# Attention with sinks and routed experts on one core: transpositions of P on half of the array, the sinks' exponentials apart from P, x stored in whole rows

## The chip, the cores and the metric

One of the eight cores of a Trainium2 chip runs the kernel. A core has TensorE (matmuls and weight loads, results in PSUM), VectorE, ScalarE, GpSimd and SyncE, which here issues transfers; in the profile they are PE and PEld, DVE, ACT, POOL and SP. The metric is the device time of one execution in microseconds.

## The reference

Causal attention in a window of 128 positions, to which the first four positions (the sinks) are always added, and behind it a layer of eight experts. An expert takes 384 of the 3072 tokens, in the order of the routing logits.

```python
batch, n_heads, seq, head_dim = (4, 8, 768, 64); n_sink, window = (4, 128)
scores = scale * np.matmul(q, k.transpose(0, 1, 3, 2))
keep = is_sink | in_window
scores = np.where(keep, scores, -1000000000.0)
a = np.exp(scores - np.max(scores, axis=-1, keepdims=True))
a = a / (np.sum(a, axis=-1, keepdims=True) + 1e-09)
x = np.matmul(a, v)                    # (B, H, S, D), then (B*S, H*D)
logits = x @ w_gate                    # N=3072, D=512, E=8
# each token goes to its best expert that still has room (cap = N // E)
h = np.maximum(x[mask] @ w1[e], 0.0)   # F=1024
out[mask] = h @ w2[e]
```

All data are float32.

## The kernel before

Attention comes first, then routing and experts (class `Moe`); x goes between them through DRAM (`x_dram`), the logits through the SBUF tensor `L`.

Attention works in 24 chunks of 128 queries, six for each of four batches. A chunk `c` passes these steps; `g` is one of two halves of the heads, so most of them come twice a chunk.

- `ldq`, `ldk`, `lv`: SyncE loads q, k and v, four chunks ahead. In `kk` a block of 128 keys has the four sinks' keys in front of it, `W=132` columns.
- `qs` (GpSimd, L74): q times 0.125.
- `QK` (TensorE, L83): the scores into a PSUM tile `pp`, as 64x64 matmuls on the four quarters of the array. Because one query half of 64 sees the keys from its own diagonal back, a row has 64 columns of an older block, 64, the 4 sinks, and 64.
- `cp` (VectorE, L89 to L93): triangles of the two diagonal blocks are merged into 64 columns by a predicated copy; `mx` (L94) takes the maximum.
- `e` (ScalarE, L99): the exponentials of 132 columns of a head into `P`, with their sum into `sm`.
- `T` (TensorE, L107): the 64x64 blocks of P are transposed by matmuls with an identity; `pe` (ScalarE, L108) copies them into `PT`.
- `A`, `B` (GpSimd, L110, L111): the merged diagonal block is split into its two triangles, `E` and what stays in `PT`.
- `ss` (ScalarE, L114): two copies, one for each half of the queries, take the sinks' columns of P into `ss`, a tile that holds zeros for the other batches. `Ts` (TensorE, L118) transposes them, `pS` (ScalarE, L119) copies them.
- `AV` (TensorE, L129): PT and E times v. `ae` (VectorE, L132) copies it.
- `X` (TensorE, L136, L138): the sinks' part of the result, and the product with `iw`, which is an identity beside the gate's weights, so that 64 columns of x and 8 of logits come out for a head.
- `ra`, `r` (VectorE): 1 / (sum + 1e-9); `xe` (L140) multiplies by it and writes `xt`; `lm` (L142) adds the logits over the heads; `xo` (SyncE, L143) stores x.

Each step is a function `op_...`. Their order on each engine is not that of a loop: `schedule()` simulates all steps with costs in ns (`table`), the latencies `LAT`, rings of buffers (`buffers`: how many slots a tensor has, and which step frees one) and an offset for each step (`OFF`), and `plan_of` sorts the steps by the start so found. `attention` then issues them in that sequence. All PSUM tiles of attention are four slots `pp` of two banks, one step to a slot.

An f32 matmul of the program is issued as two passes, each of them a weight load and a matmul.

## Time and profile before

| | |
|---|---|
| three runs | 545.25 us median, 541.69 to 548.64 |
| the profiled execution | 545.01 us |
| its span, first to last instruction | 543.3 us |
| instructions in it | 16,624, of them 6873 matmuls and 6873 weight loads |
| TensorE's mean granted clock | 0.96 of 2.4 GHz |
| busy of the span: PE, PEld, DVE, ACT, POOL | 86%, 74%, 65%, 44%, 32% |

A time is that of one execution on the device; the span is what the trace covers of it. The shares are means over attention, routing and experts, which differ; each has to be read on its own. Matmuls overlap, so that a busy PE is not one at its peak. A wait is put down to what came last before the waiting instruction; "issue" is idle time for which the trace shows no releaser.

### The profile page before, as it was taken

The page shows a single profiled execution, that of the slowest core. Times are in us where ns is not written, and L with a number is a line of the kernel's source. Part 1 is how long each engine was busy: PE and PEld are TensorE (multiplying, and loading weights), DVE is VectorE, ACT ScalarE, POOL GpSimd, SP SyncE. Part 2 cuts the span into 40 slices and gives each one's busy share as a digit, 9 for nine tenths or more (in the row PEclk, how much of TensorE's full clock was granted, in tenths as well). Part 3 has the DMA queues.
Part 4 walks back from the last instruction along what each step waited for, and adds up shares of the span by engine and source line. Part 5 has one row for each costly group of instructions (what it writes and reads, how often), then busy time and mean ns, then how long its engine had stood idle before and what let it go on. Part 6 is the DMA issues. An engine that isn't in the chain of part 4 may idle for free.

```text
span 543.3 us, 16624 instructions
## 1 busy us (share of the span) xinstructions
PE 468.9 (86%) x6873; PEld 400.3 (74%) x6873; DVE 352.7 (65%) x1040; ACT 237.2 (44%) x690; POOL 174.0 (32%) x231
## 2 busy tenths in 40 slices
PE   7777776877777478898999998999999989999995
...
GB/s 237 201 171 167 167 140 159 160 160 167 83 74 51 32 117 246 8 187 220 21 303 85 61 326 40 74 276 79 79 329 21 180 373 184 58 21 54 25 6 53
DMA packets 75085, 73.23 MB, mean 135 GB/s; under 512 B 28033, under 2 KB 57601, under 8 KB 75009
## 3 DMA queue, kind: packets, MB, share of 16 engines
...
q8 instruction: 54, 0.88, 0.7%
q14 instruction: 23, 0.18, 0.1%
HBM read 59.57 MB, written 12.58 MB: 133 GB/s over the span
## 4 chain that ended last, share of the span: by engine, by line
PE 57%; DMA 15%; DVE 12%; issue 10%; ACT 2%; POOL 2%; SPq 1%; POOLq 0%; ACTq 0%; DVEq 0%
PE ph L680 16%; PE py L692 15%; DMA raw<-w 12%; PE pp L129 6%; PE pp L83 5%; PE pp L107 5%; PE pp L138 2%; PE pp L136 2%; PE pr L543 2%; DVE wl L654 2%; DVE cmp L473 2%; PE pt L667 1%; DMA xg<-x_dram,idx 1%; DVE hl L684 1%; DMA us<-ud 1%
## 5 line engine op out<-in xcount | busy, mean ns | idle before, releaser
L652 ACT ACTIVATE wh<-raw 128x1024 fp32r<-128x1024 f32 x64 | 67.8, 1060 | 76.9 <-DMA raw<-w 38.9
L680 PE MATMUL ph<-xh,wh 128*128 128x384 f32 x256 | 92.3, 360 | 4.0 <-DVE hl L684 4.0
L654 DVE TENSOR_TENSOR wl<-raw,wh 128x1024 fp32r<-128x1024 f32 x64 | 77.7, 1220 | 23.2 <-ACT wh L652 22.9
L680 PE MATMUL ph<-xl,wh 128*128 128x384 f32 x256 | 88.1, 344 | 0.0
L680 PE MATMUL ph<-xh,wl 128*128 128x384 f32 x256 | 88.0, 344 | 0.0
L692 PE MATMUL py<-wh,hh 128*128 128x512 f32 x192 | 79.9, 416 | 2.2 <-ACT yo L695 2.2
L697 POOL DMA_INDIRECT out<-yo,idx x24 | 26.7, 1114 | 166.9 <-ACT yo L695 113.4
L659 POOL DMA_INDIRECT xg<-x_dram,idx x24 | 33.3, 1389 | 139.5 <-issue 49.5
L692 PE MATMUL py<-wh,hl 128*128 128x512 f32 x192 | 75.9, 395 | 0.0
L692 PE MATMUL py<-wl,hh 128*128 128x512 f32 x192 | 75.8, 395 | 0.0
L99 ACT ACTIVATE P<-pp,nmx 128x132 f32<-128x132 f32 x192 | 69.0, 372 | 7.9 <-DVE nmx L94 6.6
L683 ACT ACTIVATE hh<-ph 128x384 fp32r<-128x384 f32 x64 | 31.2, 488 | 82.3 <-PE ph L680 61.7
L684 DVE SCALAR_TENSOR_TENSOR hl<-ph,hh 128x384 fp32r<-128x384 f32 x64 | 35.3, 553 | 39.7 <-ACT hh L683 39.1
L107 PE MATMUL pp<-idt,P 64*64 64x64 f32 x1536 | 39.6, 226 | 23.5 <-issue 23.5
L680 PEld LDWEIGHTS ph<-xh,wh 128*128 128x128 f32 x256 | 50.2, 196 | 7.1 <-DVE hl L684 5.1
L107 PEld LDWEIGHTS pp<-idt,P 64*64 64x64 f32 x1536 | 35.0, 140 | 24.0 <-issue 23.5
L110 POOL TENSOR_TENSOR E<-PT,me 128x256 f32<-128x256 f32 x48 | 35.7, 744 | 49.2 <-ACT PT L108 48.6
L680 PEld LDWEIGHTS ph<-xl,wh 128*128 128x128 f32 x256 | 49.6, 194 | 2.0
L680 PEld LDWEIGHTS ph<-xh,wl 128*128 128x128 f32 x256 | 49.6, 194 | 0.0
L83 PE MATMUL pp<-kk,q 64*64 64x196 f32 (+2 forms) x768 | 44.5, 327 | 4.8 <-issue 3.5
L108 ACT ACTIVATE PT<-pp 128x512 f32<-128x512 f32 x48 | 28.6, 597 | 33.1 <-PE pp L107 32.9
L692 PEld LDWEIGHTS py<-wh,hh 128*128 128x128 f32 x192 | 36.9, 192 | 7.6 <-ACT yo L695 2.6
...
## 6 DMA issues: line engine op xcount, KB each, us to landing
...
v<-vd SPq DMA_DIRECT2D x24, 256.0 KB, 3.8
x_dram<-xt SPq DMA_DIRECT2D x24, 256.0 KB, 3.1
...
q<-qd SPq DMA_DIRECT2D x23, 256.0 KB, 4.9
xg<-x_dram,idx POOLq DMA_INDIRECT x24, 5.8
out<-yo,idx POOLq DMA_INDIRECT x24, 2.8
...
```

Source lines behind the costliest of these rows:

```text
L83: PE.matmul(sp[o,s,196*u+a:196*u+196],q[p,g+2*u,o],kk[p,g+2*u,k0+64*f+a:k0+64*f+196],start=True,stop=True)
L99: A.activation(T('P',c)[:,h,:],sp[:,s,u,64:196],AF.Exp,bias=T('nmx',c)[:,b:b+1],scale=1.0,accum_out=T('sm',c)[:,h:h+1])
L107: for u in range(2): PE.matmul(t[half(u),s,128*x+64*l:128*x+64*l+64],T('P',c)[half(s),2*(g+2*u)+x,a:a+64],idn[half(s),half(s)],start=True, ...
L110: def op_A(c,g): G.tensor_tensor(T('E',c)[:,2*g:2*g+2],diag(c,g),me[:,None].to_broadcast([128,2,2,64]),OP.mult)
L129: PE.matmul(av[half(s),u,a:a+64*n],T('v',c-w)[half(u),256*l+64*x:256*l+64*x+64],m.rearrange("p a n->p (a n)"),start=g==0 and n==2 and w==0 ...
L652: g.add('A',947,lambda wh=wh,raw=raw: nc.scalar.activation(wh,raw,AF.Copy),[f'raw{q}'],[f'wh{s}'],f'H{k}.{j}',f'W{k}')
L654: g.add(e,{'V':1135,'P':2303}[e],lambda wh=wh,wl=wl,raw=raw,e=e: (nc.vector if e=='V' else nc.gpsimd).tensor_tensor(wl,raw,wh.bitcast(F32) ...
L659: g.add('P',1038,lambda t=t: nc.gpsimd.indirect_dma_start(out=self.xg[t],out_offset=None,in_=self.x_dram,in_offset=bass.IndirectOffsetOnAx ...
L680: nc.tensor.matmul(p[:,0:CAP],x[:,c,:],y[:,c,:],start=c==0 and i==0,stop=c==3 and i==2)
L683: g.add('A',371,lambda f=f,p=p: nc.scalar.activation(self.hh[:,f,:],p[:,0:CAP],AF.Relu),ps,[f'hh{f}'],f'hh{k}.{f}',f'H{k}')
L684: g.add('V',469,lambda f=f,p=p: nc.vector.scalar_tensor_tensor(self.hl[:,f,:],p[:,0:CAP],0.0,self.hh[:,f,:].bitcast(F32),op0=OP.max,op1=OP ...
L692: nc.tensor.matmul(p,x[:,f,ts],w,start=f==0 and i==0,stop=f==7 and i==2)
```

## The change

Three things are done, and the plan is computed anew for them.

First, `T`. P is laid out so that two heads' blocks of 64 columns lie side by side, and one transposition takes both: 64 rows and 128 columns of the array, written to all 128 partitions, instead of two f32 matmuls with the identity. `Ts` does the same.

Second, the sinks. They are no longer part of P. The keys lie as 4 sinks, 64 keys, 4 sinks, 64 keys (`W=136`), so that every query half finds the sinks between its two blocks of scores. A new step `sd` on VectorE subtracts the maximum from the four columns, `ss` is one exponential on ScalarE from there, with no copy from P; a new step `rs` on VectorE sums the sinks' exponentials, and `ra` adds that to the sum of the rest.

Third, `xt` holds 512 columns of x and behind them 64 of logits. `xe` writes them with two instructions, and `xo` stores rows of 2 KB where it stored pieces of 256 bytes.

`schedule()` gets new costs, a cost for changes of the array's shape (`SWITCH`), and for each 256 instructions of TensorE a least distance (`INS`, `FETCH`); `OFF` is a new table, of which the diff shows one line.

```diff
-W=132
+W=136
...
-    for n,sh,dt in (('v',[128,512],F32),('P',[128,H,W],F32),('nmx',[128,H],F32),('sm',[128,H],F32),('PT',[128,4,4,64],F32),('E',[128,4,2,64],F32),
-                    ('pS',[128,128],F32),('r',[128,H],F32),('at',[128,HP,128],F32),('xt',[128,H,72],F32)):
+    for n,sh,dt in (('v',[128,512],F32),('P',[128,4,2,2,64],F32),('sd',[128,2,HP,4],F32),('nmx',[128,H],F32),('sm',[128,H],F32),('PT',[128,4,4,64],F32),('E',[128,4,2,64],F32),
+                    ('pS',[128,128],F32),('r',[128,H],F32),('at',[128,HP,128],F32),('xt',[128,576],F32)):
...
-                    p,o=half(s),half(f); a=0 if i else 64 if f else 128
-                    PE.matmul(sp[o,s,196*u+a:196*u+196],q[p,g+2*u,o],kk[p,g+2*u,k0+64*f+a:k0+64*f+196],start=True,stop=True)
+                    p,o=half(s),half(f); a=0 if i else 68 if f else 132; k0=(i-1)*W+4+68*f
+                    PE.matmul(sp[o,s,200*u+a:200*u+200],q[p,g+2*u,o],kk[p,g+2*u,k0+a:k0+200],start=True,stop=True)
...
+    def op_sd(c,g):
+
+        V.tensor_tensor(T('sd',c)[:,:,g::2,:],scores(c,g)[:,:,:,132:136],nmx(c,g)[:,:,:,None].to_broadcast([128,2,2,4]),OP.add)
     def op_e(c,x):
         g,u=x//2,x%2; sp=scores(c,g)
         for s in range(2):
             h=2*(g+2*u)+s; b=4*g+2*s+u
-            A.activation(T('P',c)[:,h,:],sp[:,s,u,64:196],AF.Exp,bias=T('nmx',c)[:,b:b+1],scale=1.0,accum_out=T('sm',c)[:,h:h+1])
+            A.activation(T('P',c)[:,2*g+s,:,u,:],sp[:,s,u,64:200].rearrange("p (a n)->p a n",a=2)[:,:,4:68],AF.Exp,bias=T('nmx',c)[:,b:b+1],scale=1.0,accum_out=T('sm',c)[:,h:h+1])
     def op_T(c,g):
 
         t=T('p',c,f'T{g}')
         for x in range(2):
             for l in range(2):
                 for s in range(2):
-                    a=((68,0),(4,68))[s][l]
-                    for u in range(2): PE.matmul(t[half(u),s,128*x+64*l:128*x+64*l+64],T('P',c)[half(s),2*(g+2*u)+x,a:a+64],idn[half(s),half(s)],start=True,stop=True)
+                    PE.transpose(t[:,s,128*x+64*l:128*x+64*l+64],T('P',c)[half(s),2*g+x,1-(l^s)].rearrange("p u n->p (u n)"),idn[half(s),half(s)])
...
-    def op_ss(c):
-        for f,a in ((0,64),(1,0)): A.activation(ss(c)[half(f),:,c//NB],T('P',c)[half(f),:,a:a+4].rearrange("p (h s) k->p s h k",s=2),AF.Copy)
+    def op_ss(c): A.activation(ss(c)[:,:,c//NB],T('sd',c),AF.Exp)
     def op_Ts(c):
         t=T('p',c,'Ts'); x=ss(c).rearrange("p s b h k->p (s b h k)")
         for s in range(2):
-            for r in range(2): PE.matmul(t[half(r),s,0:64],x[half(s),half(r)],idn[half(s),half(s)],start=True,stop=True)
+            PE.transpose(t[:,s,0:64],x[half(s)],idn[half(s),half(s)])
...
-    def op_ra(c): V.tensor_scalar(T('r',c),T('sm',c),1e-9,None,op0=OP.add)
+    def op_rs(c): V.tensor_reduce(T('r',c).rearrange("p (j s)->p s j",s=2),ss(c)[:,:,c//NB],AX.X,OP.add)
+    def op_ra(c): V.scalar_tensor_tensor(T('r',c),T('r',c),1e-9,T('sm',c),op0=OP.add,op1=OP.add)
...
-        V.tensor_tensor(T('xt',c).rearrange("p (j s) n->p s j n",s=2),T('p',c,'X')[:,:,0:288].rearrange("p s (j n)->p s j n",j=4),
-            T('r',c).rearrange("p (j s)->p s j",s=2)[:,:,:,None].to_broadcast([128,2,4,72]),OP.mult)
...
+        for a,b,n in ((0,64,0),(64,72,512)):
+            V.tensor_tensor(T('xt',c)[:,n:n+8*(b-a)].rearrange("p (j s n)->p s j n",s=2,j=4),x[:,:,:,a:b],r.to_broadcast([128,2,4,b-a]),OP.mult)
...
+    def op_xo(c): nc.sync.dma_start(x_dram[c*128:(c+1)*128,:],T('xt',c)[:,0:512])
...
-    add('ss','A',260,ae+[('~zs',1-NB)])
-    add('ra','V',75,ae)
+    add('ss','A',140,[('sd0',0),('sd1',0)]+[('~zs',1-NB)])
+    add('rs','V',100,[('ss',0)])
+    add('ra','V',75,ae+[('rs',0)])
...
+                if ins[0]>=256:
+                    w=max(0,ins[1]+FETCH-(t1-cost*(ins[0]-256)/INS[k])); t1+=w; ins[1]=t1-cost*(ins[0]-256)/INS[k]; ins[0]-=256
...
-SWITCH=dict(nr=90,rn=200)
+SWITCH=dict(nr=90,rn=200,nt=90,tn=200,rt=100,tr=200)
+INS=dict(QK0=32,QK1=32,T0=16,T1=16,Ts=4,AV0=64,AV1=64,X=80,U=16); FETCH=4300
...
-OFF={'A0': 18335, 'A1': 52415, 'AV0': 14908, 'AV1': 84106, 'B0': 47216, 'B1': 7783, 'QK0': 2872, 'QK1': 4297, 'T0': 8328, 'T1': -8153, 'Ts': 15650, 'U': -22652, 'Uc': -13081, 'cp0': -10470, 'cp1': 78107, 'e0': 58010, 'e1': 95573, 'e2': 687, 'e3': 927, 'fi': 95598, 'lm': -9483, 'mx0': 14597, 'mx1': -49747, 'pS': 60593, 'pe0': 61206, 'pe1': -9424, 'pr0': 95367, 'pr1': -19606, 'pr10': -47988, 'pr11': 79834, 'pr12': 60010, 'pr13': -8724, 'pr14': 3651, 'pr15': 2764, 'pr2': 75294, 'pr3': -25455, 'pr4': 59901, 'pr5': -70, 'pr6': 12471, 'pr7': 98043, 'pr8': -8311, 'pr9': 6044, 'qs': 50785, 'r': 61220, 'ra': -6513, 'ss': 79894, 'um': 11705, 'xe': -10955, 'xo': -20341, 'zs': -5463, 'pr16': -102190, 'ae': -9891, 'X': -32988}
```

TensorE in the midst of attention, before (a row is a matmul of the program, `x16` sixteen alike; `pp_...` is a PSUM slot; `kk,q` is QK, `idt,P` T, `vx,pS` and `iw,at` X, `PT,v` and `E,v` AV, `idt,ss` Ts):

```order
L83 MATMUL pp_214<-kk,q_166 64x196 x8
L107 MATMUL pp_216<-idt,P_245 64x64 x16
L136 MATMUL pp_215<-vx,pS_263 64x288 x4
L138 MATMUL pp_215<-iw,at_270 64x72 x16
L107 MATMUL pp_213<-idt,P_245 64x64 x16
L83 MATMUL pp_216<-kk,q_166 64x196 x8
L129 MATMUL pp_215<-PT_256,v_241 64x128 x4
L129 MATMUL pp_215<-PT_256,v_239 64x128 x4
L129 MATMUL pp_215<-E_259,v_239 64x64 x4
L129 MATMUL pp_215<-E_259,v_241 64x64 x4
L118 MATMUL pp_213<-idt,ss_2_232 64x64 x4
```

The same place after:

```order
L130 MATMUL pp_213<-PT_259,v_240 64x128 x4
L130 MATMUL pp_213<-PT_259,v_241 64x128 x4
L130 MATMUL pp_213<-E_263,v_241 64x64 x4
L130 MATMUL pp_213<-E_263,v_240 64x64 x4
L138 MATMUL pp_216<-vx,pS_266 64x288 x4
L140 MATMUL pp_216<-iw,at_272 64x72 x16
L109 MATMUL pp_214<-idt,P_245 128x64 x8
L82 MATMUL pp_213<-kk,q_162 64x200 x8
L109 MATMUL pp_214<-idt,P_245 128x64 x8
L119 MATMUL pp_216<-idt,ss_2_229 128x64 x2
L82 MATMUL pp_215<-kk,q_162 64x200 x8
```

X has left its place between the two T; the second T has Ts right behind it, and the two AV stand together, so that the array's shape changes four times a chunk: before and behind the first T, and around the second with Ts.

VectorE, before, from one `xe` to the next:

```order
L140 TENSOR_TENSOR xt_272<-pp_215,r_267 128x2x4x72
L142 TENSOR_REDUCE L<-xt_272 128x8
L89 COPY_PREDICATED pp_213<-mprev,pp_213 128x2x2x64
L94 TENSOR_REDUCE nmx_250<-pp_213 128x4
L132 COPY at_270<-pp_215 128x512
L89 COPY_PREDICATED pp_214<-mprev,pp_214 128x2x2x64
L94 TENSOR_REDUCE nmx_249<-pp_214 128x4
L130 TENSOR_SCALAR r_267<-sm_254 128x8
L131 RECIPROCAL r_267<-r_267 128x8
```

The same place after, as far as the next `xe`:

```order
L144 TENSOR_TENSOR xt_276<-pp_215,r_267 128x2x4x64
L144 TENSOR_TENSOR xt_276<-pp_215,r_267 128x2x4x8
L131 TENSOR_REDUCE r_268<-ss_1_231 128x2x4
L145 TENSOR_REDUCE L<-xt_276 128x8
L88 COPY_PREDICATED pp_213<-mprev,pp_213 128x2x2x64
L94 TENSOR_REDUCE nmx_253<-pp_213 128x4
L88 COPY_PREDICATED pp_215<-mprev,pp_215 128x2x2x64
L97 TENSOR_TENSOR sd_248<-pp_213,nmx_253 128x4x4
L94 TENSOR_REDUCE nmx_253<-pp_215 128x4
```

The step `sd` (L97) stands behind the copy of the next scores, not right behind its own maximum; `rs` (L131) has come in, and `xe` is two rows.

## Rows read from the trace of the kernel before

**Rows 1.** Busy times of two stretches, from the first restart of TensorE after a gap to the routing, and from there to the end. Columns: the stretch, its length, then for each engine the busy time and (x) its instructions, the granted clock of TensorE as a share of 2.4 GHz, the share of the DMA engines, GB/s.

```profile
18.64:176.08 157.44, 117.34 (x4670) 106.94 (x4670) 102.86 (x233) 105.64 (x468) 101.63 (x128) 0.99 0.49 135
176.08:543.30 367.22, 337.30 (x1985) 284.49 (x1984) 241.41 (x787) 122.50 (x184) 60.06 (x48) 0.95 0.37 128
```

**Rows 2.** What TensorE's matmul row waited for in attention: engine, tile and line, the releaser, us in total, times, longest.

```profile
PE pp L107 <- issue: 23.5, 17, 2.2
PE pp L138 <- issue: 5.4, 4, 1.9
PE pp L129 <- issue: 4.8, 9, 1.2
PE pp L83 <- issue: 3.5, 3, 2.3
PE pp L129 <- POOL PT L111: 1.0, 1, 1.0
```

**Rows 3.** Busy times of stretches, each from one restart of TensorE after a gap of issue to a later one; columns as in rows 1. First single ones, then longer ones (of 8, 10, 11 and 5 such steps), and the whole.

```profile
83.46:88.56 5.10, 2.83 (x129) 2.62 (x129) 2.77 (x8) 3.71 (x17) 4.06 (x5) 1.00 0.71 202
...
102.44:106.68 4.24, 3.42 (x127) 3.09 (x127) 2.78 (x6) 2.99 (x14) 3.17 (x7) 1.00 0.76 195
...
140.16:144.05 3.89, 3.04 (x128) 2.72 (x127) 2.11 (x5) 2.95 (x12) 2.44 (x3) 1.00 0.09 21
...
18.64:53.15 34.51, 25.00 (x1018) 22.59 (x1018) 22.06 (x49) 24.89 (x112) 26.49 (x32) 1.00 0.55 158
58.25:102.44 44.19, 32.73 (x1274) 29.94 (x1274) 27.30 (x60) 30.19 (x133) 29.98 (x41) 0.96 0.53 148
102.44:148.15 45.71, 35.32 (x1401) 32.01 (x1401) 31.39 (x67) 32.61 (x145) 31.51 (x39) 1.00 0.53 143
148.15:168.83 20.68, 15.55 (x637) 14.32 (x637) 13.83 (x38) 13.80 (x61) 8.91 (x13) 1.00 0.27 67
...
18.64:168.83 150.19, 111.98 (x4457) 102.08 (x4457) 98.04 (x222) 104.59 (x465) 99.83 (x126) 0.99 0.51 140
```

**Rows 4.** The page's part on DMA queues: queue and kind, packets, MB, share of 16 engines; the row of TensorE's instruction blocks.

```profile
q8 instruction: 54, 0.88, 0.7%
```

**Rows 5.** Groups of instructions by line up to 220 us, shapes kept apart: T (L107) and Ts (L118), matmuls (PE; weight loads have rows of their own, PEld, with the same counts). Columns: line, engine, operation, out<-in, rows*columns of the array, moving or loaded operand, xcount | busy us, mean ns of one | idle before.

```profile
L107 PE MATMUL pp<-idt,P 64*64 64x64 f32 x1536 | 39.6, 226 | 23.5 <-issue 23.5
...
L118 PE MATMUL pp<-idt,ss 64*64 64x64 f32 x192 | 9.1, 222 | 1.5 <-ACT P L99 0.9 <-issue 0.7
```

**Rows 6.** Timeline of TensorE's matmuls in a stretch with no gap, nearly a chunk: start us, us from the first start to the last end, line, tiles, shape, count.

```profile
97.45 0.61 PE L129 MATMUL pp<-PT,v 64*64 64x128 f32 x16
...
98.11 0.29 PE L118 MATMUL pp<-idt,ss 64*64 64x64 f32 x8
98.23 0.61 PE L129 MATMUL pp<-PT,v 64*64 64x128 f32 x16
...
98.90 0.84 PE L83 MATMUL pp<-kk,q 64*64 64x196 f32 x16
99.57 0.64 PE L107 MATMUL pp<-idt,P 64*64 64x64 f32 x32
100.03 0.66 PE L136 MATMUL pp<-vx,pS 64*64 64x288 f32 x8
...
101.02 0.28 PE L107 MATMUL pp<-idt,P 64*64 64x64 f32 x6
```

**Rows 7.** Transpositions of f32 in the expert stage (L667): the weight loads of those that write to pt, 90 of 96 (ns, min/median/max), and six of them in the timeline.

```profile
L667 PEld LDWEIGHTS pt<-idt,xg x90: 138/140/229, 204.2 to 464.4; 128*128 128x128 f32 x90
...
409.17 0.85 PE L667 MATMUL pt<-idt,xg 128*128 128x128 f32 x6
```

**Rows 8.** Timeline of TensorE's weight loads at two changes between 64x64 and the full array, and the group of L69's loads.

```profile
6.78 0.33 PEld L149 LDWEIGHTS <-const-float32-0.0 128*128 128x128 bf16 x3 [0.18 <-issue]
...
11.11 0.42 PEld L69 LDWEIGHTS pp<-us 128*128 128x128 f32 x3
11.55 0.21 PEld L83 LDWEIGHTS pp<-kk,q 64*64 64x64 f32 x8
...
L69 PEld LDWEIGHTS pp<-us 128*128 128x128 f32 x8 | 1.0, 191 | 2.1 <-DMA us<-ud 2.1
```

**Rows 9.** Groups of the other engines in attention (columns as in rows 5): GpSimd, ScalarE's sink copy, VectorE's nearest small ones.

```profile
L110 POOL TENSOR_TENSOR E<-PT,me 128x256 f32<-128x256 f32 x48 | 35.7, 744 | 49.2 <-ACT PT L108 48.6
...
L74 POOL TENSOR_SCALAR q<-q 128x512 f32<-128x512 f32 x23 | 34.5, 1501 | 4.1 <-DMA q<-qd 4.1
...
L114 ACT ACTIVATE ss<-P 64x32 f32<-64x32 f32 x48 | 10.7, 222 | 0.3
...
L142 DVE TENSOR_REDUCE L<-xt 128x8 f32<-128x64 f32 x24 | 6.5, 269 | 0.6
...
L90 DVE COPY_PREDICATED pp<-m,big 128x16 f32<-128x16 int32 x8 | 1.7, 214 | 0.3
```

**Rows 10.** DMA issues of the page: what, KB each, us to landing.

```profile
x_dram<-xt SPq DMA_DIRECT2D x24, 256.0 KB, 3.1
```

**Rows 11.** The clock: busy times of two stretches (columns as in rows 1), and the start of T in the second in the timeline; X runs from 93.64 us to there.

```profile
86.29:93.64 7.35, 3.03 (x129) 2.90 (x127) 4.34 (x11) 3.46 (x18) 4.08 (x5) 1.00 0.53 148
93.64:97.08 3.44, 3.44 (x82) 2.86 (x85) 1.06 (x3) 2.06 (x8) 1.45 (x2) 0.51 0.02 5
...
95.57 1.09 PE L107 MATMUL pp<-idt,P 64*64 64x64 f32 x32
```

More of the change, by code (lines that the diff above doesn't have):

```diff
@@ L77, in op_QK @@
         i=c%NB; q=qs[c%NQ]; sp=T('p',c,f'QK{g}')
-        k0=(i-1)*W+4 if i else -128
         for u in range(2):
@@ L159, in layouts @@
     sk=np.broadcast_to(kT[:,:,:,None,:4],(B,H,64,NB,4))
-    kd=pairs(np.concatenate([sk,kT.reshape(B,H,64,NB,128)],-1))
+    kb=kT.reshape(B,H,64,NB,2,64)
+    kd=pairs(np.concatenate([sk,kb[:,:,:,:,0],sk,kb[:,:,:,:,1]],-1))
     vd=v.reshape(B,2,4,NB,2,64,64).transpose(1,5,0,3,4,2,6).reshape(128,B,NB,512)
@@ L186, in table @@
     for h in range(2):
-        add(f'QK{h}','E',lambda c: 660 if c%NB else 445,[('ldk',0),('ldk',-1),('qs',0)]+[(f'{n}{x}',0) for x in ((0,1),(2,))[h] for n in ('qs.','ldk')])
+        add(f'QK{h}','E',lambda c: 675 if c%NB else 445,[('ldk',0),('ldk',-1),('qs',0)]+[(f'{n}{x}',0) for x in ((0,1),(2,))[h] for n in ('qs.','ldk')])
         add(f'cp{h}','V',lambda c: 335 if c%NB>1 else 490 if c%NB else 670,[(f'QK{h}',0)])
         add(f'mx{h}','V',615,[(f'cp{h}',0)])
-        for u in range(2): add(f'e{2*h+u}','A',697,[(f'mx{h}',0)])
+        add(f'sd{h}','V',95,[(f'mx{h}',0)])
+        for u in range(2): add(f'e{2*h+u}','A',690,[(f'mx{h}',0)])
     ae=[(f'e{h}',0) for h in range(4)]
     for g in range(2):
-        add(f'T{g}','E',490,[(f'e{2*g}',0),(f'e{2*g+1}',0),('ldn',0)])
+        add(f'T{g}','E',250,[(f'e{2*g}',0),(f'e{2*g+1}',0),('ldn',0)])
         add(f'pe{g}','A',479,[(f'T{g}',0)])
@@ L197, in table @@
     add('zs','P',lambda c: 480 if c%NB==1 and c//NB<B-1 else None,[('B1',0)])
-    add('ss','A',260,ae+[('~zs',1-NB)])
-    add('ra','V',75,ae)
+    add('ss','A',140,[('sd0',0),('sd1',0)]+[('~zs',1-NB)])
+    add('rs','V',100,[('ss',0)])
+    add('ra','V',75,ae+[('rs',0)])
     add('r','V',120,[('ra',0)])
-    add('Ts','E',130,[('ss',0),('ldn',0)])
+    add('Ts','E',65,[('ss',0),('ldn',0)])
     add('pS','A',230,[('Ts',0)])
@@ L210, in table @@
     add('X','E',980,[('ae',0),('pS',0),('um',0),('ldi',0)])
-    add('xe','V',680,[('X',0),('r',0)])
+    add('xe','V',740,[('X',0),('r',0)])
     add('lm','V',135,[('xe',0)])
@@ L267, in schedule @@
                 for x in rs: readers[x,c].append((t,k,c))
-    et=collections.defaultdict(float); et['E']=3700.0; mode=['n']; out=[]; ld=[]; fills=[]; dq=[0.0]
+    et=collections.defaultdict(float); et['E']=3700.0; mode=['n']; ins=[100,0.0]; out=[]; ld=[]; fills=[]; dq=[0.0]
     def dma(t,dur):
@@ L321, in schedule @@
             if e=='E':
-                md='n' if k=='U' else 'r'
-                t1+=SWITCH.get(mode[0]+md,0); mode[0]=md
+                md='n' if k=='U' else 't' if k[0]=='T' else 'r'
+                t1+=SWITCH.get(mode[0]+md,0); mode[0]=md; ins[0]+=INS[k]//(2 if k[:2]=='AV' and c%NB==0 else 1)
+                if ins[0]>=256:
+                    w=max(0,ins[1]+FETCH-(t1-cost*(ins[0]-256)/INS[k])); t1+=w; ins[1]=t1-cost*(ins[0]-256)/INS[k]; ins[0]-=256
             if e=='E' and s<60000 and s-et[e]>400:
@@ L764, in attention_general @@
                     sp=ps.tile([128,384],F32,name="sp",bufs=2)
-                    nc.tensor.matmul(sp,q[hs,h//2,:],kT[hs,h//2,3*g:3*g+3,4:W],start=True,stop=True)
+                    nc.tensor.matmul(sp,q[hs,h//2,:],kT[hs,h//2,3*g:3*g+3].rearrange("p b (l w)->p b l w",l=2)[:,:,:,4:68],start=True,stop=True)
                     nc.scalar.activation(sc[:,384*g:384*g+384],sp,AF.Copy,scale=0.125)
```

30 lines of the change are left out of this document (16 added, 14 removed).

## The prediction

> **What bounds the kernel now.** The change touches only the attention stage, so I read its length first. By the busy times of two stretches [rows 1] it ends near 176 us, where the routing begins; the 367.22 us behind that are expert work, whose code is the same. In attention the matmul row of TensorE is busy 117.34 of 157.44 us and no other engine more, so none is full. The next view is what TensorE waited for [rows 2]: hardly any of it is another engine (GpSimd has most, 1.0 us). Nearly all is "issue", idle time with no releaser: 23.5 + 5.4 + 4.8 + 3.5 us and some smaller, about 38 us.
>
> What "issue" is shows when stretches are cut from one restart of TensorE after such a gap to the next [rows 3]. Whatever lies in them, matmuls and weight loads together come to 254 to 258, and each stretch takes 3.89 to 5.10 us though the matmuls are busy in only 2.83 to 3.42 us of it. A gap every 256 instructions is no dependency of the program. The table of DMA queues has the partner [rows 4]: 54 instruction packets of 0.88 MB together, 16 KB each, and 13,746 matmuls and weight loads are 54 times 256. So TensorE runs through a block of 256 instructions and then stands until the next has been fetched. The last row of [rows 3] holds 35 blocks: 150.19 us / 35 = **4.29 us a block**, which is what sets the pace of attention. Its 8914 counted instructions are 255 a block; the rest are semaphore instructions, which that view leaves out.
>
> **The change, part by part.** *Transposes.* Before, T costs 1536 matmuls and as many loads in 24 chunks, 64 + 64 a chunk, Ts 8 + 8 [rows 5]: an f32 matmul is issued as two passes of a load and a matmul. A transposition of the array is one load and one matmul: L667 makes 12 for each of 8 experts, 90 of the 96 into pt, and these have 90 loads [rows 7]. The new T makes 8 of them for each half of a chunk, Ts 2: 32 + 4 instructions instead of 128 + 16. That is 108 fewer a chunk; a full chunk of 416 comes to 308 by my count (the title says 304, which I don't find).
>
> *Blocks.* The chunk that lies before 18.64 us is left out. 23 chunks x 108 / 255 = 9.7 blocks fewer, x 4.29 us = **41.8 us less**, if each block still takes 4.29 us. About 27 blocks are left to attention. The four stretches at the foot of [rows 3] hold 8, 10, 11 and 5 blocks: 4.31, 4.42, 4.16 and 4.14 us a block. With 4.14 for all the time falls by 4 us more, with 4.42 by 3.5 us less; I take the mean.
>
> *What is late next.* A full chunk of 308 instructions is 1.21 blocks, 5.18 us by the fetch. On the array a chunk now takes 4.70 us where nothing stops it [rows 6]: two AVs and Ts 1.45 us (97.45 to 98.90), one QK 0.67, one T 0.46, X 0.99 (100.03 to 101.02), and QK and T once more. Without T and Ts (0.92 + 0.12) that is 3.66 us. The new T isn't in the trace. Nearest is L667, six f32 transpositions in 0.85 us of which the last lasts 0.27 [rows 7]: 0.116 us each, on the full array with 128 columns. Eight one behind the other would be 0.93 us; but the new ones take turns between the two halves of the array's rows, as the old four-way ones overlap in quarters, and at two at a time they take 0.46 us, the old figure. At the old pace per instruction (0.46 us for 32 pairs) they would be 0.12 us. I take 0.46 us; two and a Ts are 1.04 us. New, too, is the change of shape, 64x64 to 64x128 and back, four a chunk by the order above. The nearest rows change between the full array and 64x64 [rows 8]. Into the full array the loads stand still for 0.18 us ahead of 6.78 us. Out of it, three loads fill 11.11 to 11.53 us, each 0.19 us long, so they start 0.115 us apart and the last at 11.34; the next starts at 11.55 us, 0.21 us later, so 0.10 us are lost. Four cost 0.40 to 0.72 us; nothing of the trace excludes 0. I take 0.5 us. Then the array needs 3.66 + 1.04 + 0.5 = 5.2 us a chunk, as much as the fetch. Of a fetch of 4.29 us TensorE idles 1.4 us now, which swallows every late input; that cover is gone afterwards.
>
> *The other engines* [rows 9]. GpSimd keeps its work: 1.50 + 4 x 0.74 = 4.46 us a chunk (L111 is as long as L110). ScalarE loses one of two sink copies (0.22 us), and its exponentials are 128 columns wide, not 132. VectorE gets two sd, one rs and a second piece of xe; the nearest rows are 0.22 us (L90, 16 columns in PSUM) to 0.27 us (L142), so about 0.9 us more on the 102.86 us / 23 chunks = 4.5 us that it is busy now [rows 1]. Those 5.4 us overlap in part (a next instruction starts before the recorded end of the last), but on ss, rs, ra and r now hangs xe, which frees the PSUM tile of X, and sd is one reader more that has to leave the tile of QK. All three engines would be 75 to 95% busy in a chunk of 5.5 us.
>
> Two demands of 5.2 us a chunk that vary (blocks from 3.89 to 5.10 us), with three engines close behind, don't give 5.2 us together. My estimate is 0.25 us a block over the fetch, 4.54 us, that is 5.5 us a full chunk: 27 x 0.25 = **6.8 us given back**. Its ends are 0 and the array's upper bound, which is a rival.
>
> *The x store.* 24 transfers in pieces of 256 bytes land in 3.1 us [rows 10]; now 2 KB each. The store lies on no wait of [rows 2]; that the last rows arrive sooner ends beside the routing, and the gathers that read them start at 199 us. Fewer packets may shorten the fetch, which shares the DMA engines: at most the 4 us above. The keys grow from 528 to 544 bytes a piece, 3%. I take 0 for both.
>
> **Sum.** The profiled execution took 545.01 us, span 543.3 us; the median of the three runs is 545.25, so the two need no correction. 545.0 - 41.8 + 6.8 = **510.0 us**. The bounds of the terms: 545.0 - 41.8 = 503 without anything given back, 499 with blocks of 4.14 us.
>
> **Rivals.** *The array becomes the bound.* Transpositions that don't overlap (2 x 0.93 + 0.23 us) and changes of shape at 0.18 us each make 3.66 + 2.09 + 0.72 = 6.47 us a full chunk. From 18.64 us on there are 23 chunks; the four of 24 that open a batch have half the AV, 64 instructions fewer, so a mean chunk is 297.3 / 308 = 0.965 of a full one. 23 x 0.965 x 6.47 = 143.6 us, 13.8 us less than the 157.44 us of now: 531 us. For it: the two rows of another shape are all there is. Against: the 32 pairs of the old T, on four quarters of the array, take 0.46 us together [rows 6], so pieces of the array do overlap. Chance 0.17.
>
> *Another engine or a chain sets the pace.* GpSimd at 4.46 us plus its waits for ScalarE, or VectorE with its additions, at 6.0 us a full chunk: 23 x 0.965 x 6.0 = 133.2 us, 521 us. Against: before the change they deliver whenever a block comes early, after 3.89 us. Chance 0.08.
>
> *The clock falls; slower.* The row of the clock is 1.00 through nearly all of attention; it was 0.51 (1.2 GHz instead of 2.4) from 93.64 to 97.08 us, after a stretch with TensorE busy 3.03 of 7.35 us [rows 11]. At that clock X takes 1.93 us (93.64 to 95.57) for 0.99: 1.9 times as long. If the new mix ran at 1.2 GHz throughout, a chunk would be 1.9 x 5.2 = 9.9 us, 23 x 0.965 x 9.9 = 220 us, the end at 607 us; it costs more than the fetch gives back from about a third of the time at that clock on. Against it: the matmuls that stay, 3.66 us, come in a shorter chunk than now, so they stand closer. Chance 0.04. The Trainium skill speaks for this rival ("TensorE: Matmul & The Clock Gate", Part 4: PE-mode transpose): it says that the full clock isn't engaged by transpositions. No run here shows a long row of them.
>
> *The gaps are no fetch; slower.* If their cause lay elsewhere and 38 us of gaps stayed, fewer instructions would save nothing, and the array's 5.2 instead of 4.70 us a chunk would add 23 x 0.5 = 11.5 us: 556 us. Against it stands the count of 256. Chance 0.03. The Trainium skill has it so ("Runtime: NRT & Kernel Launch", Instruction fetch mechanics): it holds that TensorE's instructions are read in 16 KB blocks and that this is hidden, since instructions are issued more slowly than blocks arrive. The size agrees with [rows 4], the hiding does not: 4.29 us a block against 2.9 us of work (256/416 of 4.70). By that sentence the time would be 545 us or above.
>
> **How the numbers follow.** The forecast, 499 to 518 us, has 0.65; the array 0.17, another engine 0.08, the clock 0.04, no fetch 0.03, and 0.03 is for what I don't see. The range is 499 to 524 us: it holds the forecast, the engine case and the lower part of the array case. Two per cent, about what a measurement of this kernel tells from no change, is 534 us. Faster by that has 0.65 + 0.08 and most of the array case, 0.89 in all; within 2% the rest of it, 0.05; slower 0.06.
>
> **What the profile after would show.** Instruction packets fall from 54 to about 44. The routing begins near 141 us, not 176. "Issue" on TensorE falls to less than half of 38 us, and between restarts there are still 256 instructions, at 4.1 to 4.6 us a block. T with its eight matmuls takes 0.4 to 0.5 us with its gaps at the changes of shape beside it; GpSimd is the fullest of the others. If T stands at 0.9 us and the gaps at its edges at 0.2 us, the array case holds; if the clock's digits in attention fall, that one; if the gaps no longer come at every 256th instruction but the time is the same, my reading of them is wrong.

## The result and the profile after

The changed kernel takes **518.34 us** (median of 4 runs, 517.38 to 518.71) where the kernel before took 546.19 us in runs on the same chip (median of 4): a ratio of 0.950, with a 95% interval from 0.943 to 0.956. It is faster by 5%, inside the range of the forecast (499 to 524 us), 8.3 us above the forecast of 510.0 us and 0.3 us above the 499 to 518 us that had most of the chance. The profiled execution took 518.64 us, its span is 516.9 us.

The two stretches of [rows 1], cut again at the routing, show where the time went. Columns: stretch, length, then busy time and (x) instructions of TensorE's matmuls, its weight loads, VectorE, ScalarE and GpSimd, the granted clock, DMA share, GB/s.

```profile
18.64:152.36 133.72, 114.91 (x3445) 92.47 (x3435) 112.85 (x325) 98.98 (x447) 99.53 (x128) 1.00 0.52 160
152.36:516.90 364.54, 335.77 (x1985) 283.55 (x1985) 241.18 (x787) 122.39 (x184) 62.90 (x48) 0.96 0.37 129
```

Attention ends 23.7 us earlier (152.36 us, not 176.08). The rest is 2.7 us shorter, though its code is the same; with that code it took between 364.4 and 371.9 us in the profiled executions below, so this difference is no effect of the change. TensorE's matmuls are now busy for 86% of attention (75% before), VectorE for 84% (65%). The clock stayed at 1.00, that is 2.4 GHz.

The row of instruction packets [rows 4]:

```profile
q8 instruction: 44, 0.72, 0.6%
```

The stops of the kernel before follow these packets. Between 18.64 and 176.08 us its trace puts 30 idle times of TensorE's matmuls of 0.3 us or more down to "issue", and each of them ends 1.2 to 1.6 us after an instruction packet has arrived. In the changed kernel four are left, 1.4 to 1.5 us after a packet.

And what TensorE's matmuls waited for in attention, the view of [rows 2] (releaser: us in total, times, longest):

```profile
PE pp L109 <- ACT P L102: 10.1, 13, 1.5
PE pp L119 <- DVE at L134: 1.9, 1, 1.9
PE pp L109 <- DVE xt L144: 1.4, 3, 0.5
PE pp L82 <- issue: 1.3, 4, 0.5
PE pp L140 <- issue: 0.7, 1, 0.7
PE pp L130 <- issue: 0.7, 1, 0.7
```

"Issue" was 38 us and is now under 3. In its place stands a wait that was not there: T (L109) waits 10.1 us for ScalarE's exponentials (P, L102).

T itself, in the timeline of TensorE (start us, us from first start to last end, line, shape, count; before: [rows 6]):

```profile
85.48 0.46 PE L109 MATMUL pp<-idt,P 64*128 64x64 f32 x8
85.78 0.23 PE L119 MATMUL pp<-idt,ss 64*128 64x64 f32 x2
85.93 0.91 PE L82 MATMUL pp<-kk,q 64*64 64x200 f32 x16
...
88.64 0.46 PE L109 MATMUL pp<-idt,P 64*128 64x64 f32 x8
89.03 0.89 PE L82 MATMUL pp<-kk,q 64*64 64x200 f32 x13
```

Eight transpositions, then Ts 0.30 us later (so, or a little sooner, in 9 of the 14 cases up to 142 us; 0.40 to 0.75 us in the others), and the next 64x64 work 0.16 to 0.21 us after Ts. Where 64x64 work follows T itself, it starts 0.39 to 0.40 us behind T's start in 9 of 18 cases, later in the others.

### The profile page after: what moved, and what is told of

The parts are those of the page before. It is cut to its first block, busy times and chain, and to the rows that moved or that the text cites. A ratio compares the mean times of both kernels' runs of the same rounds, so it can differ in the third digit from the quotient of the medians.

```text
span 516.9 us, 14206 instructions
## 1 busy us (share of the span) xinstructions
PE 465.7 (90%) x5577; PEld 383.8 (74%) x5577; DVE 362.9 (70%) x1136; ACT 229.8 (44%) x666; POOL 175.7 (34%) x231
## 4 chain that ended last, share of the span: by engine, by line
PE 46%; DVE 16%; DMA 15%; ACT 5%; issue 3%; POOL 1%; SPq 0%; POOLq 0%; ACTq 0%; DVEq 0%
PE ph L689 17%; PE py L701 16%; DMA raw<-w 12%; ACT P L102 3%; PE pp L82 3%; DMA xg<-x_dram,idx 3%; PE pr L552 2%; PE pp L130 2%; PE pt L676 2%; DVE cmp L482 2%; PE pp L109 1%; DVE wl L663 1%; DVE nmx L94 1%; DVE hl L693 1%; ACT wh L661 1%
## 5 line engine op out<-in xcount | busy, mean ns | idle before, releaser
L706 POOL DMA_INDIRECT out<-yo,idx x24 | 28.0, 1167 | 163.9 <-ACT yo L704 115.1
L668 POOL DMA_INDIRECT xg<-x_dram,idx x24 | 34.9, 1453 | 139.0 <-issue 48.3
L102 ACT ACTIVATE P<-pp,nmx 128x128 f32<-128x128 f32 x192 | 68.4, 369 | 20.1 <-DVE sd L97 10.7
L82 PE MATMUL pp<-kk,q 64*64 64x200 f32 (+2 forms) x768 | 44.8, 333 | 2.9 <-issue 1.3
L112 POOL TENSOR_TENSOR E<-PT,me 128x256 f32<-128x256 f32 x48 | 35.4, 744 | 26.3 <-ACT PT L110 25.4
L701 PEld LDWEIGHTS py<-wh,hl 128*128 128x128 f32 x192 | 36.0, 188 | 8.1
L704 ACT ACTIVATE yo<-py 128x512 f32<-128x512 f32 x24 | 14.3, 597 | 57.4 <-PE py L701 42.4
L102 ACT ACTIVATION_READ_ACCUMULATOR P<-pp,nmx 128x1 f32 x192 | 39.4, 205 | 0.0
```

The lines of the kernel that those rows point to most:

```text
L82: PE.matmul(sp[o,s,200*u+a:200*u+200],q[p,g+2*u,o],kk[p,g+2*u,k0+a:k0+200],start=True,stop=True)
L102: A.activation(T('P',c)[:,2*g+s,:,u,:],sp[:,s,u,64:200].rearrange("p (a n)->p a n",a=2)[:,:,4:68],AF.Exp,bias=T('nmx',c)[:,b:b+1],scale=1. ...
L112: def op_A(c,g): G.tensor_tensor(T('E',c)[:,2*g:2*g+2],diag(c,g),me[:,None].to_broadcast([128,2,2,64]),OP.mult)
L668: g.add('P',1038,lambda t=t: nc.gpsimd.indirect_dma_start(out=self.xg[t],out_offset=None,in_=self.x_dram,in_offset=bass.IndirectOffsetOnAx ...
L701: nc.tensor.matmul(p,x[:,f,ts],w,start=f==0 and i==0,stop=f==7 and i==2)
L704: g.add('A',478,lambda p=p,y=y: nc.scalar.activation(y,p,AF.Copy),ps,[f'yo{n%3}'],f'y{k}.{t}',f'Y{k}')
```

## The cost of sd, in the rows of after

ScalarE's waits for VectorE in attention, and VectorE's wait the other way (releaser: us in total, times, longest):

```profile
ACT P L102 <- DVE sd L97: 10.3, 25, 0.9
ACT P L102 <- DVE nmx L94: 8.4, 12, 1.2
...
DVE sd L97 <- ACT P L102: 6.5, 15, 0.7
```

The exponentials wait for sd, and sd waits for exponentials, though neither reads what the other writes. What they share is what they read: the maximum, and the PSUM tile of the scores. By these waits whichever engine comes second in the written order waits until the other has read. That it is the PSUM tile and not the maximum, the runs below show. One such place in the timeline (start us, duration, engine, line, [idle before <- releaser]):

```profile
74.06 0.71 DVE L94 TENSOR_REDUCE nmx<-pp 128x4 f32<-128x528 f32 x1
...
74.68 0.90 DVE L91 COPY_PREDICATED pp<-m,big 128x256 f32<-128x256 int32 x1
...
74.86 0.37 ACT L102 ACTIVATE P<-pp,nmx 128x128 f32<-128x128 f32 x1 [1.21 <-DVE nmx L94]
...
75.22 0.36 ACT L102 ACTIVATE P<-pp,nmx 128x128 f32<-128x128 f32 x1
...
75.62 0.83 DVE L92 COPY_PREDICATED pp<-mf,big 128x256 f32<-128x256 int32 x1
76.36 0.16 DVE L97 TENSOR_TENSOR sd<-pp,nmx 128x16 f32<-128x16 f32 x1
...
76.56 0.37 ACT L102 ACTIVATE P<-pp,nmx 128x128 f32<-128x128 f32 x1 [0.89 <-DVE sd L97]
...
77.42 0.46 PE L109 MATMUL pp<-idt,P 64*128 64x64 f32 x8 [1.44 <-ACT P L102]
```

The maximum is there at 74.77 us and the first two exponentials of the half follow. The other two could start at 75.6. They start at 76.56, because sd comes ahead of them in the order, and sd stands on VectorE behind two mask copies for the other half. TensorE's T waits 1.44 us for them, and about 1.0 us of that (75.58 to 76.56) is their wait for sd. An instruction of 0.16 us costs that much by where it stands. Whether this is the missing gain, the runs below say. The Trainium skill gives a reason for such an order ("PSUM — Partial Sum Buffer", PSUM bank collisions raise a hardware error): the chip doesn't put two engines' accesses to one bank and quadrant one behind the other but reports an error, so the compiler's scheduler adds a dependency between them, ScalarE against VectorE and reads against reads too. The 25 + 15 waits look like such dependencies; which part of the software sets them here, no run shows.

## Experiments

Routing times below are the first matmul of the routing in each profiled execution; the changed kernel has 152.36 us. They come from one execution each. In some of these TensorE's clock was granted at half for a stretch of about 3.4 us in attention, which I estimate to cost 1.7 us at most (X takes 1.93 us for 0.99 at that clock [rows 11]); it is said where a comparison hangs on it.

### T in two passes again

```
-  PE.transpose(t[:,s,128*x+64*l:128*x+64*l+64],T('P',c)[half(s),2*g+x,1-(l^s)].rearrange("p u n->p (u n)"),idn[half(s),half(s)])
+  for u in range(2): PE.matmul(t[half(u),s,128*x+64*l:128*x+64*l+64],T('P',c)[half(s),2*g+x,1-(l^s),u],idn[half(s),half(s)],start=True,stop=True)
```

> The changed kernel with one part undone: each of the eight transposes of a T is again two ordinary f32 matmuls of 64 rows on a 64x64 quarter, in the changed kernel's order and with everything else (sinks' exp apart, x rows, score layout) as changed. TensorE instructions a chunk: 308 + 96 = 404. Fetch theory (TensorE is paced by its instruction packets, 4.29 us a block of 256): packets of the instruction queue 44 -> 53, TensorE stops again at every 256th instruction, 404/255 x 4.29 = 6.8 us a chunk instead of 5.6, 24 x 1.2 = 29 us more: 547 us (541 to 552). Array theory (only the array's own time counts): the eight transposes' 0.46 us become about 0.93, 24 x 2 x 0.47 = 22 us more: 540 us, with no stops at every 256th instruction. The two times lie near each other; the stops and the next run tell them apart.

Measured: 544.2 us (one run), routing at 170.56 us. Three stretches from one restart of TensorE to the next, the whole stretch, the largest waits of TensorE and the packets:

```profile
79.94:83.83 3.89, 3.09 (x128) 2.70 (x127) 3.54 (x10) 3.00 (x15) 2.76 (x3) 1.00 0.30 89
83.83:88.54 4.71, 3.12 (x128) 2.83 (x127) 4.10 (x11) 3.17 (x15) 3.32 (x4) 1.00 0.50 164
88.54:93.20 4.66, 3.73 (x126) 3.15 (x127) 3.27 (x8) 2.77 (x12) 2.84 (x5) 1.00 0.83 234
18.64:170.56 151.92, 124.90 (x4525) 106.03 (x4526) 114.08 (x324) 100.16 (x447) 99.20 (x128) 0.99 0.46 142
...
PE pp L130 <- issue: 7.1, 8, 1.6
PE pp L109 <- issue: 6.5, 9, 1.7
...
q8 instruction: 53, 0.87, 0.7%
```

With 96 instructions a chunk back, the stops are back, again 253 to 255 matmuls and loads apart, and with them 25.9 us on the total. Attention is 18.2 us longer; the rest took 371.9 us here, the longest of all, which is no effect of the edit. The 9051 matmuls and loads of the stretch are 35.5 blocks of 255, 4.28 us each, the pace of the kernel before. So 18.2 of the 23.7 us by which attention got shorter hang on T's 96 instructions a chunk (one stretch at half the clock lies in this run, 19.3 to 22.7 us, as one does in the kernel before). The other 5.5 us are still there in this run; Ts's 12 instructions a chunk make 23 x 12 / 255 x 4.29 = 4.6 us of them by the same pace, and little is left for the rest of the change. sd is in this run too, but T waits only 2.1 us for the exponentials (10.1 without the stops): the stops covered most of it. The time alone lies between both theories' (547 and 540); the stops and the pace decide for the fetch.

### 96 empty instructions a chunk

```
+            if k[:2] in ('QK','AV'):
+                for _ in range(24): PE.nop(hint='pad',nofuse=True)
```

> The changed kernel with 96 empty instructions a chunk added to TensorE's stream (24 behind each QK0, QK1, AV0 and AV1), which give the array nothing to do; nothing else differs, the output too. Instructions a chunk 308 + 96 = 404, as with the transposes undone. Fetch theory: the same time as with the transposes undone, 547 us (541 to 556), with stops at every 256th instruction, the empty ones counted, and 53 instruction packets. Array theory: the array's work is unchanged, so the time stays near 518 us (up to 525 if handing out an empty instruction takes a few ns that nothing hides).

Measured: 639.5 us, outside both theories. The timeline behind one AV, and attention as a whole:

```profile
154.79 0.47 PE L130 MATMUL pp<-E,v 64*64 64x64 f32 x8
156.15 1.24 PE L138 MATMUL pp<-vx,pS 64*64 64x288 f32 x8 [0.89 <-issue]
...
18.64:271.80 253.16, 173.49 (x3488) 130.62 (x3489) 115.49 (x331) 102.09 (x455) 101.85 (x130) 0.73 0.29 87
```

24 empty instructions leave the array idle for 0.89 us here, 37 ns each; not at all four places of a chunk, since all idle time put down to "issue" is about 40 us. In all, the matmuls stand idle for 79.7 us of attention, 18.8 us in the changed kernel. With the array idle so often, the granted clock was 0.73 on average instead of 1.00, and nearly the same number of matmuls was busy for 173.5 us, not 114.9. The test was badly chosen: it measures the price of empty instructions, not that of a fetch, and decides nothing.

### The kernel before with more work for the array

```
-  for u in range(2): PE.matmul(t[half(u),s,a:a+64],P_half,idn[half(s),half(s)],start=True,stop=True)
+  k=2-x; i=idn[half(s),half(s)][:,None].to_broadcast([64,k,64])
+  for u in range(2): PE.matmul(t[half(u),s].rearrange("p (k n)->p k n",k=2)[:,0:k,a:a+64],P_half,i,start=True,stop=True)
```

(a is 128x+64l, P_half the same slice of P in both.)

> The kernel before with more array time and no instruction more: half of the transposes' matmuls move the identity twice (128 columns in place of 64, the second copy written beside the first and read by nobody). That is 2 x 16 passes of 64 columns a chunk; by the 0.93 us that sixteen such matmuls, 32 passes, take, 0.85 us a chunk of array time, 20 us in all. Fetch theory (the kernel before is paced by its instruction packets and the array has 1 us a chunk to spare): 0 to +5 us against the kernel before, 54 packets, shorter stops at every 256th instruction. Array theory: +16 to +22 us.

Measured: 546.76 us (median of 10) beside 544.70 us for the kernel before (median of 12), ratio 1.005 (1.0005 to 1.009); routing at 175.92 us, before 176.08. T's matmuls in attention, one T and the instruction behind it, the whole stretch, the packets:

```profile
L108 PE MATMUL pp<-idt,P 64*64 64x128 f32 x720 | 34.8, 275 | 6.9 <-issue 6.9
L108 PE MATMUL pp<-idt,P 64*64 64x64 f32 x725 | 24.9, 220 | 10.4 <-issue 10.4
...
99.39 0.84 PE L108 MATMUL pp<-idt,P 64*64 64x128 f32 x30
100.06 0.41 PE L137 MATMUL pp<-vx,pS 64*64 64x288 f32 x1
...
18.64:175.92 157.28, 126.57 (x4670) 118.65 (x4668) 103.19 (x231) 105.66 (x467) 100.25 (x128) 0.98 0.50 135
...
q8 instruction: 54, 0.88, 0.7%
```

A T now holds the array for 0.67 us (99.39 to 100.06) where it held it for 0.46 [rows 6]: the added work is 0.21 us each, half of what I had put down, 24 x 2 x 0.21 = 10 us. The busy time of the matmuls grew by 9.2 us against [rows 1]. Nothing of that reached the end of attention, and 2.7 us the total by the ratio (0.3 to 5.1). Work that fits into the stops is free for attention; that is the fetch theory, from the other side.

### x in pieces of 256 bytes again

```
-  for a,b,n in ((0,64,0),(64,72,512)): V.tensor_tensor(xt[:,n:n+8*(b-a)]..., x[:,:,:,a:b], r.to_broadcast([128,2,4,b-a]),OP.mult)
+  V.tensor_tensor(xt.rearrange("p (j s) n->p s j n",s=2), x, r.to_broadcast([128,2,4,72]),OP.mult)
-  nc.sync.dma_start(x_dram[c*128:(c+1)*128,:],T('xt',c)[:,0:512])
+  nc.sync.dma_start(x_dram[c*128:(c+1)*128,:].rearrange("p (h d)->p h d",h=H),T('xt',c)[:,:,0:64])
```

> The changed kernel with the third part undone: x goes out in pieces of 256 bytes again, from one multiplication a chunk (xe) instead of two; order and everything else as changed. If the store's form is worth nothing and VectorE's second xe instruction costs its place (it starts 0.13 us behind the first), 24 x 0.13 = 3 us less at most: 515 to 519 us. If the 25,000 small packets of the kernel before were a burden on the loads, 2 to 8 us more than 518. The forecast took this part at 0.

Measured: 520.44 us (517.12 to 523.54), routing at 153.20 us. The store lands in 2.8 us (2.1 with rows of 2 KB, 3.1 in [rows 10]):

```profile
x_dram<-xt SPq DMA_DIRECT2D x24, 256.0 KB, 2.8
```

The median lies at the edge of the second expectation, but the range covers the changed kernel's. The edit also undoes xe's second instruction, so a loss by the store and a gain by xe may hide each other: xe waits 1.6 us for the store here, not at all in the changed kernel. What the runs tell is that the two together are worth nothing that can be told from 0.

### sd without the scores' tile, three ways

The first takes the scores from a constant in SBUF, the second both operands, so that it doesn't wait for the maximum either.

```
-  V.tensor_tensor(T('sd',c)[:,:,g::2,:],scores(c,g)[:,:,:,132:136],nmx(c,g)...,OP.add)
+  V.tensor_tensor(T('sd',c)[:,:,g::2,:],big[:,0:16]...,nmx(c,g)...,OP.add)         (first)
+  V.tensor_tensor(T('sd',c)[:,:,g::2,:],big[:,0:16]...,big[:,16:20]...,OP.add)     (second)
+  V.tensor_reduce(T('sd',c)[:,:,g::2,:],nmx(c,g)[:,:,:,None,None].to_broadcast([128,2,2,4,1]),AX.X,OP.add)  (third)
```

> The changed kernel, but sd (the sinks' scores less the maximum) takes its scores from a constant in SBUF and not from the scores' PSUM tile; so the sinks' part of the output is left out. VectorE's work is the same, in the same place. What goes is the order between sd and the exponentials on one PSUM tile (the second pair of exponentials waits for sd, and sd for the first pair). Chain theory (this to and fro is why the gain was 28 us and not 35): routing begins 4 to 11 us earlier than 152.4 us, total 508 to 514 us, and ScalarE's wait for sd, 10.3 us, is gone. Array theory (the array with its changes of shape takes 5.6 us a chunk): 517 to 520 us, TensorE's waits for P turn into other waits. Work theory (VectorE's added work sets it): 517 to 520 us too, and the next run falls.

> The changed kernel, but sd adds two constants from SBUF: the same 48 instructions on VectorE in the same places, which wait neither for the scores' tile nor for the maximum; the sinks' part of the output is left out. It lies between the run with sd from SBUF and the maximum (routing at 148.9 us) and the one without sd (141.9 us), and splits their 7.0 us. If VectorE's stand until the maximum is done is what costs (sd starts 742 ns behind the maximum's start where another instruction starts 625 ns behind it): routing at 142 to 145 us, total 509 to 513 us. If it is the instruction itself (its 92 ns of place, 48 times 4.4 us) or that the sinks' exponential waits for sd: routing at 146 to 149 us, total 513 to 517 us.

Measured: the first 516.60 us (513.69 to 518.42), routing at 148.90; the second 516.97 us (514.82 to 521.61), routing at 150.59. That is less than the chain theory wants, and the second is no faster than the first; its routing lies outside both of its expectations. In the first, which still reads the maximum, the exponentials' waits for sd and sd's for them are gone; in the second two waits for sd are left, 2.0 us together. The row of sd itself, in the changed kernel, the first and the second, gives a reason for the small gain (busy us, mean ns | idle before):

```profile
L97 DVE TENSOR_TENSOR sd<-pp,nmx 128x16 f32<-128x16 f32 x44 | 7.5, 171 | 7.0 <-ACT P L102 6.5
...
L97 DVE TENSOR_TENSOR sd<-big,nmx 128x16 f32<-128x16 f32 x43 | 15.2, 354 | 0.4
...
L97 DVE TENSOR_TENSOR sd<-big 128x16 f32<-128x16 f32 x43 | 14.0, 327 | 0.0
```

With two operands in SBUF sd is twice as long: the edit took one cost away and put another, 48 x 0.18 = 8.8 us of VectorE, in its place. Their routing times hold a second one: TensorE's clock was granted at half, 1.2 GHz, in two stretches of attention of 3.4 us in either run. The two of the first:

```profile
43.40:46.80 3.40, 3.40 (x50) 2.37 (x46) 2.39 (x10) 2.48 (x11) 2.41 (x4) 0.50 0.52 159
77.50:80.90 3.40, 3.40 (x50) 2.37 (x46) 2.35 (x6) 2.60 (x12) 2.01 (x3) 0.50 0.94 290
```

Whether the longer sd brought these about isn't shown. Hence the third form, whose one operand is the maximum:

> A cleaner form of the run with sd from SBUF, whose sd turned out to take 0.36 us in place of 0.17, since both its operands lay in SBUF: here sd is a reduction over one element of the maximum (one operand in SBUF, as rs has, 0.18 us), in the same place, and it still waits for the maximum; the scores' PSUM tile is not read, and the sinks' part of the output is left out. It splits the 10.5 us that sd costs: if the order against the exponentials on the PSUM tile is most of it, routing at 142 to 146 us, total 508 to 513 us; if sd's place on VectorE and its stand behind the maximum are, 148 to 152 us, 514 to 519 us.

Measured: **509.66 us** (507.18 to 512.25), routing at **144.06 us**. Its attention, its sd, and ScalarE's largest wait for VectorE:

```profile
18.64:144.06 125.42, 112.59 (x3414) 91.52 (x3415) 110.78 (x322) 95.52 (x440) 98.92 (x127) 1.00 0.55 171
...
L97 DVE TENSOR_REDUCE sd<-nmx 128x16 f32<-128x16 f32 x43 | 7.0, 164 | 0.5
...
ACT P L102 <- DVE nmx L94: 12.8, 18, 1.2
```

The same length, the same place, the same wait for the maximum; only the scores' tile isn't read. The waits between sd and the exponentials are gone, and attention ends 8.3 us earlier, with the clock at 1.00 in both.

### No sd at all

```
-        else: ops[k[:-1]](c,int(k[-1]))
+        elif k[:2]!='sd': ops[k[:-1]](c,int(k[-1]))
+    for t in R['sd']: G.memset(t,-50.0)
```

> The changed kernel with the 48 sd instructions left out (sd is set once, at the start, to -50), so the sinks' part of the output is left out; the rest and its order are the same. Chain theory: as with sd read from SBUF, within 2 us (508 to 514). Work theory (VectorE's 48 x 0.17 us is what is missing): 4 to 8 us earlier than the run with sd from SBUF. Array theory: 517 to 520 us.

Measured: 511.27 us (509.50 to 516.68), routing at 141.86 us.

```profile
18.64:141.86 123.22, 113.01 (x3414) 91.78 (x3414) 107.06 (x279) 95.10 (x440) 98.92 (x127) 0.99 0.56 174
```

All of sd is worth 10.5 us of attention in this profile, and up to 1.7 more, since the clock was granted at half from 105.50 to 108.90 us; 8.3 are the order on the PSUM tile. What lies between this run and the one before would be sd's own place on VectorE; the medians (511.3 and 509.7) don't show it. Beside the first form attention ends 7.0 us earlier, which by the expectation spoke for the work theory; the third form, with 48 instructions as long as sd's, answers that. The matmuls are busy 92% of this stretch.

### Versions that move sd's reading to ScalarE

ScalarE copies the sinks' scores out of PSUM, in its own queue beside the exponentials; then no second engine reads the tile behind the maximum. The maximum is taken off once a chunk, from SBUF, on GpSimd in the first version and on VectorE in the second. The table of numbers that sets the order was searched anew for each.

```
-    def op_sd(c,g): V.tensor_tensor(T('sd',c)[:,:,g::2,:],scores(c,g)[:,:,:,132:136],nmx(c,g)...,OP.add)
+    def op_sc(c,g): A.activation(T('sc',c)[:,:,g::2,:],scores(c,g)[:,:,:,132:136],AF.Copy)
+    def op_sd(c): G.tensor_tensor(T('sd',c)...,T('sc',c)...,T('nmx',c)[:,:,None].to_broadcast([128,8,4]),OP.add)     (first; V. in the second)
```

> A version meant to beat both: the sinks' scores are copied out of PSUM by ScalarE (16 columns for each half of the heads, in its own queue beside the exponentials, so that no other engine reads that PSUM tile between them), and the maximum is taken off on GpSimd, one instruction of 128x32 a chunk; VectorE has no sd. The order of all engines is planned anew for this. The output is whole. Theory (sd on VectorE, with its wait for the maximum and its order against the exponentials, costs 10.5 us): most of the 10.5 us are gained, routing begins at 142 to 147 us, total 508 to 513 us. If the place in the chain is not what counts, or ScalarE's two copies (about 0.12 us each) and GpSimd's add weigh as much: 516 to 522 us.

> As the version with the sinks' copies on ScalarE, but the maximum is taken off on VectorE, one instruction of 128x32 a chunk from SBUF, not on GpSimd, and the order planned anew. The output is whole. If GpSimd (27.5 of 30 us busy there) now holds that version up: routing earlier than 146.0 us, 142 to 145, total 505 to 510 us. If VectorE's place is dearer than GpSimd's: 512 to 516 us.

Measured: the first 512.13 us (509.17 to 514.49), routing at 146.01, ratio to the kernel before 0.935 (0.929 to 0.942). The second **508.34 us** (507.20 to 509.32), routing at 142.82, ratio **0.932** (0.928 to 0.936). The second:

```profile
18.64:142.82 124.18, 112.76 (x3413) 90.76 (x3409) 109.66 (x301) 97.63 (x485) 99.45 (x127) 1.00 0.56 172
...
L95 ACT ACTIVATE sc<-pp 128x16 f32<-128x16 f32 x44 | 8.3, 192 | 4.3 <-DVE nmx L94 4.1
...
L96 DVE TENSOR_TENSOR sd<-sc,nmx 128x32 f32<-128x32 f32 x22 | 6.1, 276 | 0.0
...
ACT P L101 <- DVE nmx L94: 5.8, 13, 1.0
```

Attention ends 9.5 us earlier than in the changed kernel, with the whole output, though ScalarE got 0.38 us a chunk more to do. The first version is 3.2 us later. That GpSimd held it up is not shown: its order is another, its clock was granted at half from 141.70 to 145.20 us, up to 1.7 us of the 3.2, and the intervals of the two ratios overlap. The second is the fastest version here with the whole output, faster than both kernels.

A control for the new order: the changed kernel's instructions with sd where it was, and only the numbers searched anew in the same way.

> A control: the changed kernel's own instructions, sd on VectorE as it is, only the table of numbers that sets the order searched anew, as was done for the two versions with the sinks' copies on ScalarE. If the new order and not the place of sd made those versions faster: 509 to 514 us. If sd's place did: 515 to 522 us, routing at 150 to 155 us.

Measured: 518.86 us (514.97 to 520.63), routing at 150.18 us. The waits are those of the changed kernel:

```profile
ACT P L102 <- DVE sd L97: 9.6, 23, 1.1
...
DVE sd L97 <- ACT P L102: 6.9, 16, 0.7
```

A new order alone gives nothing on the total, and 2.2 of the 9.5 us in attention, so it is where the scores are read that counts.

## Why the forecast was right, and where it was off

*The bound, and the blocks saved: right.* Packets fell from 54 to 44, as forecast, and matmuls and loads from 13,746 to 2 x 5577 = 11,154, by 2592 = 24 x 108. That fetch paced the kernel before is shown from three sides: its stops end 1.2 to 1.6 us after a packet's arrival, instructions put back bring the stops and the 4.28 us a block back, and array work put in without instructions is hidden (10 us in, none of it in attention). The run with the instructions put back shows that T carries 18.2 of the 23.7 us of attention.

*The array: the rival fell, and the array is cheaper than taken.* Where nothing holds it up, T takes 0.30 us, or 0.39 us with its change back; the forecast had 0.46 and the rival 0.93. Ts with its change back takes 0.16 to 0.21 us; the forecast had 0.12 us and a share of 0.5 us for four changes. Added up from stretches without a gap (94.35 to 97.73 us for two AV, two QK, T and Ts, 1.09 us from 91.51 us for X, 0.39 us for the other T), a chunk needs about 4.9 us by my estimate, not the 5.2 put down. The run without sd ends attention at 141.86 us; 27 blocks of 4.54 us from 18.64 us give 141.2.

*The give-back: the step that failed.* I put down 0.25 us a block, 6.8 us. Measured, attention after 18.64 us takes 133.72 us for 27 blocks, 4.95 us a block: 133.72 - 27 x 4.29 = 17.9 us given back, 11.1 us more than forecast. sd is 10.5 us of that in the run without it, 8.3 us by its reading of the tile alone. The forecast did say that sd "is one reader more that has to leave the tile of QK", and priced it by its busy time, 0.2 us, beside other work. What it missed is that here two readers of a PSUM tile on different engines wait for each other in the written order, so that an instruction of 0.17 us stood between the maximum and two of four exponentials, wherever VectorE had other things to do first.

*The rival of 0.08 was the better description.* "Another engine or a chain sets the pace, 6.0 us a full chunk" gave 133.2 us for attention; 133.72 were measured. It named GpSimd or VectorE's additions; it is a chain through VectorE's addition. Forecast and rival differ only in this one price, and I gave the rival too little. The time lies inside the range because the range was drawn to 524 us for the sake of that rival, and by some luck: attention ends 11.2 us later than the 141.2 us above, and 2.7 us of that went under in a shorter rest.

*x store: right so far as it goes*, nothing measurable together with xe. *The clock: right*, 1.00 throughout. *No fetch: fell*, with the stops.

*What the profile after was to show:* "issue" under half of 38 us was right and too modest, under 3 us. "Between restarts still 256 instructions" was wrong: the restarts are gone, all but a few; a block is now used up in 4.95 us where its fetch took 4.29, so it is mostly there in time. "T with its eight matmuls takes 0.4 to 0.5 us" was mostly too long. "GpSimd is the fullest of the others" was wrong: VectorE is, 112.85 us of 133.72 against 99.53.

Not settled: what sd's place on VectorE costs, and what limits the fastest version, 124.18 us / 27 = 4.60 us a block, that is about 5.6 us a full chunk where fetch needs 5.2 and the array 4.9. A kernel with T alone in one pass, sinks left in P, wasn't tried.
